# Second output projection of the last tokens by seven block products, with the weight sums made beside it

## The chip, the cores and the metric

The kernel runs on one core of one Trainium2 chip. The metric is the device time of one execution in microseconds (us), the median of three timed runs. TensorE is PE in the rows below (PEld its weight loads), VectorE is DVE, ScalarE is ACT, GpSimd is POOL; SP issues the DMAs.

## The reference, cut to what matters

```python
attn_out = _attn_ref(q, k, v)                     # window attention, 4 x 8 x 576 x 64
x = attn_out.transpose(0, 2, 1, 3).reshape(2304, 512)
h = 1.0 / (1.0 + np.exp(-(x @ moe_w_gate))) * (x @ moe_w_val)   # 2304 x 1536
x = h @ moe_w_out                                               # 2304 x 512
h = (x @ moe2_w_a) * (x @ moe2_w_b)                             # 2304 x 1536
out = h @ moe2_w_out                                            # 2304 x 512
```

Every matrix is multiplied as three products of a high and a low part (high by high, high by low, low by high), so that one 128-deep step of a product is three matmuls.

## The kernel before, in words

The 1536 hidden units are 12 blocks of 128 (`NF`). The 2304 tokens are nine blocks of 256. Five of them (`FRONT`) go through both MLPs in the first two thirds of the program, while the attention is computed and the weights are decoded from float64 words into high and low parts, which are saved to HBM (`kept`). The gate and value weights are also kept there in full precision (`kept[F, "f"]`), the output weights only as a pair (`kept[F, "o"]`).

The last four blocks, 1024 tokens, follow in a second part: first MLP (phase 0), some leftover work of token block 0, second MLP (phase 1). For each hidden block a *quad* (function `quad`) makes gate and value of the 1024 tokens by seven products of half-size blocks, each of six matmuls with 512 columns: products 1, 5, 6, 2, 7, 4, 3 in this order, into PSUM tiles `qa`, `qb`, `qc`. Between them `fill` takes jobs from the list `rest`: the output projection of the pair of hidden blocks before (`PAIR` is 2, so there are six pairs per MLP). `SLOTS` says how many jobs stand at which of the seven places. The combined weights of a quad (`wq`, made from `s`) are computed in `fetch` by POOL and ACT, some quads ahead.

In **phase 0** the projection of the first five pairs (`SEVEN`) is done by seven products as well (function `seven`): token halves x hidden blocks x halves of the output columns. It takes seven jobs for each of two row chunks, in two PSUM banks called `accx` and `accy`; a job is three matmuls of 512 columns and one or two additions of the bank to a result tile `res`, on DVE. Its operands are four sums of weights, summed earlier in `weight_sums` from high plus low and read back from HBM (`ks`), and four differences of hidden tiles (function `difference`): one DVE subtraction each, then a split into high and low by ACT and DVE (`t<-g,t`).

In **phase 1** the projection is the plain one (function `bank_sum`): for each of eight chunks of 128 tokens six matmuls with 512 columns, two hidden blocks of three, and one addition. The order of instructions on each engine is set by a scheduler from a simulated timeline; `in_order` ties PE to the order of the code, in phase 0 from its start to the sixth pair.

Of the kernel before, what the change touches and what calls it, by code (L numbers as in the profile page):

```python
# [21 lines left out]
def tile_window_attention_gated_mlps(ctx, tc, q, k, v, w1g, w1v, w1o, w2a, w2b, w2o, out):  # L22
    nc = tc.nc
    B, H, S, D = q.shape
    NT, DM = out.shape
    DFF = w1g.shape[1]
    P = 128
    NP = H // 2
    NF = DFF // P
    G = 3  # L30
    N = 256
# [3 lines left out]
    W = 2 * N  # L35
    CH = 2 * P
# [11 lines left out]
    dram = keep("dram", 1, space=bass.MemoryType.DRAM)  # L48
# [29 lines left out]
    for e in range(2):  # L78
        rows = slice(e * WIN, (e + 1) * WIN)
# [234 lines left out]
    SEVEN = NF // 2 - 1  # L314
    kept_sums = [dram.tile([P, 4, 2, CH], F32, tag=f"ks{p}", name=f"ks{p}") for p in range(SEVEN)]

    def weight_sums(p):

        fs = []
        for i in range(2):  # L320
            f = work.tile([P, DM], F32, tag="kq", bufs=3, name="oh")
            low = vs.tile([P, DM], F32, tag="v", bufs=3, name="ol")
            for j, t in enumerate((f, low)):
                nc.sync.dma_start(out=t, in_=kept[2 * p + i, "o"][:, j])
            fs.append((f, low))
# [65 lines left out]
    def decode_pair(F, i, nm):  # L391
        wf, wi = wordy.pop((F, nm))
        nc.vector.scalar_tensor_tensor(  # L393
            out=wf, in0=wf, scalar=SMALLEST, in1=wi.bitcast(F32), op0=ALU.is_ge, op1=ALU.mult
        )
        yield
        pair = wts.tile([P, 2, DM], F32R, tag=f"w{nm}", name=f"w{nm}")
        wh, wl = pair[:, 0, :], pair[:, 1, :]
        nc.scalar.activation(out=wh, in_=wf, func=AF.Copy)
        yield  # L400
        nc.vector.tensor_tensor(out=wl, in0=wf, in1=wh.bitcast(F32), op=ALU.subtract)
        parts.setdefault(F, {})[nm] = (wh, wl)
        pairs[F, nm] = pair
        yield
        if nm != "o":
            nc.sync.dma_start(out=kept[F, "f"][:, i], in_=wf)
            yield

    pairs = {}
# [244 lines left out]
    def in_order(since=0, engines=None):  # L654
        newest = {}
        for i in nc.cur_bb.bb.instructions[since:]:
# [6 lines left out]
                )  # L663
            newest[i.engine] = i.name

    def projection(ph, blk, work, begin, end):
        acc = [ps_acc.tile([P, 2, N], F32, tag="acc", name=f"acc{j}") for j in range(2)]
        for i, (w, h) in enumerate(work):
            project(ph, acc, w, h, i == 0, i == len(work) - 1)
        evacuate(ph, blk, acc, begin, end)  # L670
# [157 lines left out]

    def seven(res, begin, o, sums, b):


        half = lambda w, i: tuple(p[:, i * CH:(i + 1) * CH] for p in w)
        at = lambda i: tuple(sums[i // 2][:, i % 2, p] for p in range(2))
        a = {1: half(o[0], 0), 2: half(o[1], 0), 3: at(3), 4: half(o[1], 1), 5: at(0), 6: at(1), 7: at(2)}
        jobs = []
        for c in range(2):
            sl, bank, written = slice(c * P, (c + 1) * P), {}, set()

            def job(n, k, start, dsts, bank=bank, sl=sl, c=c, written=written):
                if k not in bank:  # L840
                    bank[k] = ps_acc.tile([P, W], F32, tag="acc", name=f"acc{k}")
                for m, (i, j) in enumerate(((0, 0), (0, 1), (1, 0))):
                    nc.tensor.matmul(  # L843
                        bank[k], lhsT=a[n][i][:, sl], rhs=b[n][j], start=start and m == 0, stop=m == 2,
                        skip_group_check=True,
                    )
                for d in dsts:
                    dst = res[d][:, c]
                    if begin and d not in written:
                        nc.scalar.activation(out=dst, in_=bank[k], func=AF.Copy)  # L850
                    else:
                        nc.vector.tensor_tensor(out=dst, in0=bank[k], in1=dst, op=ALU.add)
                    written.add(d)

            for args in (
                (1, "x", True, (0,)), (2, "y", True, (0,)), (6, "x", False, (1,)), (5, "y", True, (3,)),
                (7, "x", False, (2, 3)), (3, "y", False, (1,)), (4, "y", True, (2,)),
            ):
                jobs.append(lambda args=args, job=job: job(*args))
        return jobs  # L860

    def bank_sum(dst, pairs, begin):

# [125 lines left out]
    def fill(n=1):  # L989
        for _ in range(min(n, len(rest))):  # L990
            rest.pop(0)()
# [10 lines left out]
    PAIR = 2  # L1002
    SLOTS = {4: (1, 0, 1, 0, 1, 1, 0), 7: (0, 1, 1, 1, 2, 1, 1)}

    def slots(number):
        counts = SLOTS.get(number, (0, 0, 0, 0, number, 0, 0))
        return lambda i: fill(counts[i])

    y, hs, gs, pairs_done = {}, [], [], 0
    for n, (ph, fc) in enumerate(steps):  # L1010
        ahead(n + 1)
        w = fetched[n]
        if ph is None:
            hs.append((w, hidden(1, w, x[1, (0,)])))
            if fc == NF - 1:
                projection(1, 0, hs, False, True)
                hs = []
            continue
        if fc == 0:
            res = [accp.tile([P, 2, W], F32, tag="xacc", name=f"res{ph}{i}") for i in range(4)]  # L1020
        p = fc // PAIR
        by_seven = ph == 0 and p < SEVEN
        if by_seven and fc % PAIR == 0:
            g = quarter(0, 1, "g").bitcast(F32)
            g = [g[:, i] for i in range(2)]
            second = None
        else:
            g = [tmp.tile([P, W], F32, tag="hr", name=f"g{i}") for i in range(2)]
            second = None if by_seven else ((pairs_done - SEVEN) % 2, (fc + 1) % 2)
# [4 lines left out]
        hs.append((w["o"], quad(ph, w, x_ops, slots(number), g, second, between)))  # L1034
        if by_seven and len(hs) == 1:
            difference(ph, g[0], g[1], g[0], None)
            t1_of = lambda f=g[0]: t1.append(difference(0, f, None, None, wts.tile([P, 2, DM], F32R, tag="wa", name="t1")))
        if len(hs) < PAIR:
            continue
        if ph == 0 and p == SEVEN:  # L1040
            in_order(tied, (mybir.EngineType.PE,))
        fill(len(rest))
        pairs_done += 1
        begin, end = fc == PAIR - 1, fc == NF - 1
        if by_seven:
            sums = []
            for i in range(2):
# [9 lines left out]
            jobs = seven(res, begin, (o0, o1), sums, b)  # L1057

            def t4(before=jobs[1], b=b, args=(ph, g10, g10, g00)):
                before()  # L1060
# [60 lines left out]
```

## Time and profile before

| | us |
|---|---|
| median of three runs | 955.45 |
| lowest, highest | 952.73, 955.82 |
| the profiled execution | 954.69 |
| its span in the trace | 952.6 |
| PE busy | 936.5 |
| DVE busy | 664.8 |
| ACT busy | 469.4 |
| POOL busy | 301.9 |

The rows of the trace count from the start of the span; 2.1 us of the profiled execution lie around it. Phase 0 of the last tokens stands at about 600 to 755 us, phase 1 at about 757 to 953 us. Matmuls overlap: a row's own duration (390 ns for 512 columns) is longer than the distance from one start to the next, so the cost of a matmul is read from starts.

### The profile page before, as it was taken

How to read it: one execution, taken by the hardware profiler on the slowest of the kernel's cores; microseconds unless marked ns; L12 is line 12 of the kernel's file. 1: busy time of each engine (PE TensorE's matmuls, PEld its weight loads, DVE VectorE, ACT ScalarE, POOL GpSimd, SP SyncE). 2: the span in 40 equal slices, each digit the busy share in tenths (PEclk: the TensorE clock that was granted, in tenths of full speed). 3: DMA queues.
4: the chain of work that ended last, by engine and by line, in shares of the span. 5: the costliest groups of instructions: out<-in, count | busy, mean ns of one | idle time of the engine just before them, and what ended most of it. 6: DMA issues, size and time to landing. Idle time of an engine off the chain costs nothing.

```text
span 952.6 us, 15566 instructions
## 1 busy us (share of the span) xinstructions
PE 936.5 (98%) x5564; PEld 784.8 (82%) x5564; DVE 664.8 (70%) x1328; ACT 469.4 (49%) x1050; POOL 301.9 (32%) x318
## 2 busy tenths in 40 slices
PE   7899999999999999999999999999999999999998
PEld 6798888888888888888888888778888878888886
DVE  6997787875776874475788455788886774464655
ACT  7897555565545665544454333554433444432321
POOL 4543222332221222122013324444431435434400
PEclk9999999999999999999999999999999999999999
DMA  8987599975475754475695445555555664442212
GB/s 207 250 239 218 201 324 320 281 243 176 156 231 169 247 189 149 132 250 172 214 354 192 147 157 172 181 198 198 177 166 176 233 221 133 155 146 95 91 45 89
DMA packets 130045, 183.20 MB, mean 192 GB/s; under 512 B 62641, under 2 KB 87217, under 8 KB 129969
## 3 DMA queue, kind: packets, MB, share of 16 engines
q1 hardware_dynamic: 129968, 182.22, 59.1%
q8 instruction: 44, 0.72, 0.3%
q14 instruction: 33, 0.26, 0.1%
HBM read 117.44 MB, written 60.29 MB: 187 GB/s over the span
## 4 chain that ended last, share of the span: by engine, by line
PE 89%; DVE 5%; DMA 2%; issue 1%; POOL 1%; ACT 0%; SPq 0%; POOLq 0%; DVEq 0%; ACTq 0%
PE gps L428 15%; PE vps L428 15%; PE qa L753 13%; PE accm L528 9%; PE accq L866 8%; PE acc L481 7%; PE qb L753 7%; PE qc L753 3%; PE accy L843 3%; PE accx L843 2%; PE xps L228 2%; DMA oh<-ko 2%; PE sps L170 2%; PE tps L218 1%; POOL wi L387 1%
## 5 line engine op out<-in xcount | busy, mean ns | idle before, releaser
L387 POOL TENSOR_TENSOR wi<-wi,low 128x512 int32<-128x512 int32 x72 | 104.8, 1456 | 309.4 <-DVE wi L383 262.7
L428 PE MATMUL gps<-xh,wa 128*128 128x512 f32 (+1 forms) x584 | 169.3, 357 | 0.0
L428 PE MATMUL vps<-xh,wb 128*128 128x512 f32 (+1 forms) x584 | 167.4, 354 | 0.0
L738 POOL TENSOR_TENSOR wq<-s,wq 128x256 fp32r<-128x256 f32 x96 | 78.3, 821 | 138.3 <-ACT wq L737 138.0
L428 PEld LDWEIGHTS vps<-xh,wb 128*128 128x128 f32 x584 | 105.1, 189 | 16.1 <-ACT hr L448 0.4
L428 PEld LDWEIGHTS gps<-xh,wa 128*128 128x128 f32 x584 | 104.9, 189 | 16.0 <-issue 0.5
L428 PE MATMUL gps<-xl,wa 128*128 128x512 f32 (+1 forms) x292 | 103.0, 353 | 0.6 <-DVE xl L237 0.6
L428 PE MATMUL vps<-xl,wb 128*128 128x512 f32 (+1 forms) x292 | 102.7, 352 | 0.0
L528 PE MATMUL accm<-hh,wo 128*128 128x512 f32 (+1 forms) x296 | 83.5, 353 | 0.0
L771 ACT ACTIVATE r<-qa 128x512 f32<-128x512 f32 x72 | 42.7, 594 | 69.0 <-PE qa L753 65.7
L753 PE MATMUL qa<-op,wq 128*128 128x512 f32 x288 | 74.7, 390 | 0.7 <-ACT r L771 0.7
L481 PE MATMUL acc<-wo,hh 128*128 128x512 f32 x240 | 73.7, 392 | 0.2 <-DVE xacc L552 0.2
L753 PE MATMUL qb<-op,wq 128*128 128x512 f32 x288 | 73.6, 389 | 0.0
L393 DVE SCALAR_TENSOR_TENSOR ex<-ex,wi 128x512 f32<-128x512 f32 x72 | 49.8, 691 | 29.3 <-ACT ex L377 13.9
L735 POOL TENSOR_TENSOR s<-wf 128x256 f32<-128x256 f32 x48 | 37.5, 782 | 91.1 <-DMA wf<-kf 83.8
L753 PEld LDWEIGHTS qa<-op,wq 128*128 128x128 f32 x288 | 53.9, 188 | 12.3 <-ACT r L771 1.1
L753 PEld LDWEIGHTS qb<-op,wq 128*128 128x128 f32 x288 | 54.1, 188 | 11.2
L439 DVE SCALAR_TENSOR_TENSOR hl<-hr,hh 128x512 fp32r<-128x512 f32 (+1 forms) x73 | 48.1, 658 | 21.1 <-ACT hh L437 20.7
L437 ACT ACTIVATE hh<-hr 128x512 fp32r<-128x512 f32 (+1 forms) x73 | 40.2, 550 | 44.8 <-DVE hr L454 28.4
L428 PEld LDWEIGHTS gps<-xl,wa 128*128 128x128 f32 x292 | 55.2, 189 | 7.7 <-DVE xl L237 0.8
L428 PEld LDWEIGHTS vps<-xl,wb 128*128 128x128 f32 x292 | 55.2, 189 | 7.5
L528 PEld LDWEIGHTS accm<-hh,wo 128*128 128x128 f32 x296 | 52.7, 189 | 7.8 <-issue 0.2
(159 smaller groups left out, 1994.9 us busy)
## 6 DMA issues: line engine op xcount, KB each, us to landing
wa<-ka SPq DMA_DIRECT2D x27, 512.0 KB, 4.2
wb<-kb SPq DMA_DIRECT2D x27, 512.0 KB, 3.4
wo<-ko SPq DMA_DIRECT2D x27, 512.0 KB, 3.6
st_o<-in_moe_w_out_dram SPq DMA_DIRECT2D x24, 512.0 KB, 5.0
kf<-ex SPq DMA_DIRECT2D x48, 256.0 KB, 4.3
ka<-wa SPq DMA_DIRECT2D x24, 512.0 KB, 3.5
kb<-wb SPq DMA_DIRECT2D x24, 512.0 KB, 4.6
ko<-wo SPq DMA_DIRECT2D x24, 512.0 KB, 3.3
```

Source lines behind the costliest of these rows:

```text
L387: nc.gpsimd.tensor_tensor(out=wi, in0=wi, in1=low, op=ALU.add)
L393: nc.vector.scalar_tensor_tensor(out=wf, in0=wf, scalar=SMALLEST, in1=wi.bitcast(F32), op0=ALU.is_ge, op1=ALU.mult)
L428: nc.tensor.matmul(ps, lhsT=a[:, c * P:(c + 1) * P], rhs=b[:, c, :], start=(n == 0), stop=(n == 3 * NP - 1))
L437: nc.scalar.activation(out=hh, in_=hr, func=AF.Copy, scale=factor)
L439: nc.vector.scalar_tensor_tensor(out=hl, in0=hr, scalar=factor, in1=hh.bitcast(F32), op0=ALU.mult, op1=ALU.subtract)
L481: nc.tensor.matmul(ps, lhsT=a[:, m * P:(m + 1) * P], rhs=b, start=begin and n == 0 and (phase == 1 or m % 2 == 0), stop=end and n == 2 and ...
L528: nc.tensor.matmul(ps[:, m], lhsT=a[:, sl], rhs=b, start=k == 0, stop=k == total - 1)
L738: nc.gpsimd.tensor_tensor(out=t[:, 1], in0=s, in1=t[:, 0].bitcast(F32), op=ALU.subtract)
L753: nc.tensor.matmul(ps, lhsT=a[:, c * P:(c + 1) * P], rhs=b[:, c, :], start=first and n == 0, stop=n == 5, skip_group_check=True,)
L771: nc.scalar.activation(out=r, in_=ps, func=AF.Copy)
L843: nc.tensor.matmul(bank[k], lhsT=a[n][i][:, sl], rhs=b[n][j], start=start and m == 0, stop=m == 2, skip_group_check=True,)
L866: nc.tensor.matmul(ps, lhsT=a, rhs=b, start=n == 0, stop=n == len(pairs) - 1)
```

## The change

For the first five of the six pairs of phase 1 the projection becomes `seven` too. The tokens are the rows of the result there, so a hidden tile is the stationary operand and a block of weights, 256 columns wide, the moving one: a job is six matmuls of 256 columns, three for each of two token chunks. The sixth pair stays as it was. The differences of hidden tiles are made as in phase 0. The four sums of weights of a pair are made while its second quad runs (`sums_of`): two DMAs bring the full-precision output weights, which the decoding now writes to HBM for ten of the hidden blocks (`kept_out`), DVE makes four sums of 128x256, ACT and POOL split them. The function `behind` puts these instructions behind what stands before them in the code on their engine. PE is tied to the code's order in phase 1 also, from its second quad to its sixth pair.

```diff
+    kept_out = {F: dram.tile([P, DM], F32, tag=f"kf{F}", name=f"kf{F}") for F in range(NF, NF + 2 * SEVEN)}
...
         if nm != "o":
             nc.sync.dma_start(out=kept[F, "f"][:, i], in_=wf)
+            yield
+        elif F in kept_out:
+            nc.sync.dma_start(out=kept_out[F], in_=wf)
             yield
...
+    def behind(steps):
+        made = nc.cur_bb.bb.instructions
+        since, last = len(made), {}
+        if next(steps, steps) is steps:
+            return
+        for i in made[:since]:
+            last[i.engine] = i.name
+        for i in made[since:]:
+            if i.engine in last and i.engine != mybir.EngineType.SP:
+                tc.add_manual_dep(
...
-    def seven(res, begin, o, sums, b):
+    def seven(ph, res, begin, o, sums, b):
...
+                for r in range(2 if ph else 0):
+                    rows = slice((2 * c + r) * P, (2 * c + r + 1) * P)
+                    for m, (i, j) in enumerate(((0, 0), (0, 1), (1, 0))):
+                        nc.tensor.matmul(
+                            bank[k][:, r], lhsT=b[n][j][:, rows], rhs=a[n][i],
+                            start=start and m == 0 and r == 0, stop=m == 2, skip_group_check=True,
+                        )
                 for d in dsts:
-                    dst = res[d][:, c]
+                    i, j = divmod(d, 2)
+                    dst = res[2 * j + c][:, :, i * CH:(i + 1) * CH] if ph else res[d][:, c]
...
+    def sums_of(F):
+        p = (F - NF) // 2
+        if not spare:
+            spare.append(accp.tile([P, 2, W], F32, tag="xacc", name="osum"))
+        f = spare[0]
+        for i in range(2):
+            nc.sync.dma_start(out=f[:, i], in_=kept_out[F + i])
...
+        def steps():
+            yield
+            for n, (s, x, y, op) in enumerate((
+                (a22, a21, a22, ALU.add), (a21, a11, a21, ALU.subtract), (a11, a22, a11, ALU.subtract),
+                (a12, a12, a11, ALU.subtract),
+            )):
+                nc.vector.tensor_tensor(out=s, in0=x, in1=y, op=op)
+                if n % 2:
+                    yield
+            for n, s in enumerate((a22, a11, a21, a12)):
+                t = sums[n // 2][:, n % 2]
+                nc.scalar.activation(out=t[:, 0], in_=s, func=AF.Copy)
+                nc.gpsimd.tensor_tensor(out=t[:, 1], in0=s, in1=t[:, 0].bitcast(F32), op=ALU.subtract)
+                yield
...
+        def at(i):
+            fill(counts[i])
+            behind(also)
...
+        if fc == (1 if ph else 0):
+            tied = len(nc.cur_bb.bb.instructions)
...
-        by_seven = ph == 0 and p < SEVEN
+        by_seven = p < SEVEN
...
+        if by_seven and ph and len(hs) == 1:
+            sums, also = sums_of(NF + 2 * p)
...
-        if ph == 0 and p == SEVEN:
+        if p == SEVEN:
             in_order(tied, (mybir.EngineType.PE,))
```

Three places show what the change moves. The first is PE where phase 1 begins, in the first two quads, which have no jobs between their products. In the program before, `wq_8479` to `wq_8484` belong to the first quad, `wq_8559` to `wq_8569` to the second, `wq_8651` and `wq_8656` to the third:

```order
L753 MATMUL qa<-op_8370,wq_8479 128x512 x6
L753 MATMUL qa<-op_8375,wb 128x512 x6
L753 MATMUL qb<-op_8378,wq_8484 128x512 x6
L753 MATMUL qa<-op_8365,wq_8559 128x512 x6
L753 MATMUL qb<-op_8360,wq_8651 128x512 x6
L866 MATMUL accq<-wo,hh 128x512 x4
L753 MATMUL qc<-op_8355,wa 128x512 x6
L866 MATMUL accq<-wo,hl 128x512 x2
L753 MATMUL qa<-op_8370,wq_8564 128x512 x6
L753 MATMUL qa<-op_8352,wa 128x512 x6
L753 MATMUL qa<-op_8375,wb 128x512 x6
L753 MATMUL qb<-op_8378,wq_8569 128x512 x6
```

The same place of PE now, with `wq_8494` to `wq_8504` of the first quad and `wq_8579` to `wq_8589` of the second:

```order
L774 MATMUL qa<-op_8385,wq_8494 128x512 x6
L774 MATMUL qa<-op_8390,wq_8499 128x512 x6
L774 MATMUL qa<-op_8395,wb 128x512 x6
L774 MATMUL qa<-op_8385,wq_8579 128x512 x6
L774 MATMUL qc<-op_8375,wa 128x512 x6
L774 MATMUL qb<-op_8398,wq_8504 128x512 x6
L774 MATMUL qa<-op_8390,wq_8584 128x512 x6
L774 MATMUL qa<-op_8395,wb 128x512 x6
L774 MATMUL qb<-op_8398,wq_8589 128x512 x6
L774 MATMUL qa<-op_8372,wa 128x512 x6
```

Products of the third quad no longer stand among those of the second, whose products 7 and 4 (`wq_8584`, `wb`), both into the tile `qa`, now follow each other directly.

The second place is PE in one quad of the running phase, from its product 5 on. Before:

```order
L753 MATMUL qb<-op_8360,wq_8869 128x512 x6
L753 MATMUL qc<-op_8355,wa 128x512 x6
L753 MATMUL qa<-op_8352,wa 128x512 x4
L866 MATMUL accq<-wo,h_8638 128x512 x2
L753 MATMUL qa<-op_8370,wq_8754 128x512 x6
L866 MATMUL accq<-wo,h_8638 128x512
L866 MATMUL accq<-wo,h_8731 128x512 x3
L866 MATMUL accq<-wo,h_8638 128x512 x3
L866 MATMUL accq<-wo,h_8731 128x512 x3
L753 MATMUL qa<-op_8352,wa 128x512 x2
L753 MATMUL qa<-op_8375,wb 128x512 x6
L753 MATMUL qb<-op_8378,wq_8759 128x512 x6
```

PE in the same quad now:

```order
L774 MATMUL qb<-op_8380,wq_9107 128x512 x6
L874 MATMUL accx<-wo,hh 128x256
L874 MATMUL accx<-wo,hl 128x256
L874 MATMUL accx<-wo,hh 128x256 x2
L874 MATMUL accx<-wo,hl 128x256
L874 MATMUL accx<-wo,hh 128x256
L774 MATMUL qa<-op_8385,wq_9112 128x512 x6
L874 MATMUL accy<-wo,hh 128x256
L874 MATMUL accy<-wo,hl 128x256
L874 MATMUL accy<-wo,hh 128x256 x2
L874 MATMUL accy<-wo,hl 128x256
L874 MATMUL accy<-wo,hh 128x256
```

Groups of six 256-column matmuls stand between the products, seven groups in a quad, where groups of 512-column matmuls stood.

The third place is the end of a pair's second quad, on DVE and POOL. DVE before, from the multiplication by `qa` on:

```order
L781 TENSOR_TENSOR g_9262<-qa,g_9262 128x512
L811 TENSOR_TENSOR g_9263<-qb,r_9295 128x512
L439 SCALAR_TENSOR_TENSOR hl<-g_9262,hh 128x512
L781 TENSOR_TENSOR g_9263<-r_9318,g_9263 128x512
L801 TENSOR_TENSOR g_9387<-qc,r_9398 128x512
L870 TENSOR_TENSOR res_8574<-accq,res_8574 128x512
L439 SCALAR_TENSOR_TENSOR h_9356<-g_9263,h_9356 128x512
L870 TENSOR_TENSOR res_8574<-accq,res_8574 128x512
```

DVE now, from the same operation on:

```order
L802 TENSOR_TENSOR g_9271<-qa,g_9271 128x512
L884 TENSOR_TENSOR res_8595<-accy,res_8595 128x2x256
L444 SCALAR_TENSOR_TENSOR hl<-g_9271,hh 128x512
L832 TENSOR_TENSOR g_9272<-qb,r_9310 128x512
L884 TENSOR_TENSOR res_8593<-accy,res_8593 128x2x256
L802 TENSOR_TENSOR g_9272<-r_9344,g_9272 128x512
L840 TENSOR_TENSOR g_9125<-g_9272,g_9125 128x512 x2
L444 SCALAR_TENSOR_TENSOR h_9412<-g_9272,h_9412 128x512
L840 TENSOR_TENSOR g_9271<-g_9271,g_9125 128x512
L444 SCALAR_TENSOR_TENSOR t_9404<-g_9125,t_9404 128x512
L884 TENSOR_TENSOR res_8592<-accx,res_8592 128x2x256
L444 SCALAR_TENSOR_TENSOR t_9408<-g_9125,t_9408 128x512
```

Three subtractions (L840) and the splits of `h` and `t` now stand between the products of a pair and the first addition of the next (`res<-accx`). POOL before, making the weights of coming quads:

```order
L738 TENSOR_TENSOR wq_9369<-s_9367,wq_9369 128x256
L735 TENSOR_TENSOR s_9382<-wf,s_9372 128x256
L738 TENSOR_TENSOR wq_9374<-s_9372,wq_9374 128x256
L738 TENSOR_TENSOR wq_9379<-s_9377,wq_9379 128x256
L735 TENSOR_TENSOR s_9492<-wf 128x256
L735 TENSOR_TENSOR s_9497<-s_9492,wf 128x256
L738 TENSOR_TENSOR wq_9384<-s_9382,wq_9384 128x256
L735 TENSOR_TENSOR s_9502<-wf 128x256
L738 TENSOR_TENSOR wq_9494<-s_9492,wq_9494 128x256
```

POOL now, with the four low parts of the sums of weights (`<-osum`) among them:

```order
L756 TENSOR_TENSOR s_9438<-wf,s_9428 128x256
L923 TENSOR_TENSOR s_9275<-osum,s_9275 128x256
L759 TENSOR_TENSOR wq_9430<-s_9428,wq_9430 128x256
L756 TENSOR_TENSOR s_9569<-wf 128x256
L923 TENSOR_TENSOR s_9275<-osum,s_9275 128x256
L759 TENSOR_TENSOR wq_9435<-s_9433,wq_9435 128x256
L756 TENSOR_TENSOR s_9574<-s_9569,wf 128x256
L923 TENSOR_TENSOR s_9276<-osum,s_9276 128x256 x2
L759 TENSOR_TENSOR wq_9440<-s_9438,wq_9440 128x256
L756 TENSOR_TENSOR s_9579<-wf 128x256
```

Each pair has four such instructions more on POOL, between the weights of its coming quads.

## Rows read from the trace of the kernel before

**Rows 1.** The page: busy time of each engine over the span.
```profile
PE 936.5 (98%) x5564; PEld 784.8 (82%) x5564; DVE 664.8 (70%) x1328; ACT 469.4 (49%) x1050; POOL 301.9 (32%) x318
```

**Rows 2.** Chain that ended last, second MLP: start us, us, what.
```profile
832.27 2.72 PE accq L866 x12
...
862.19 2.72 PE accq L866 x12
```

**Rows 3.** Stretches: us; PE, PEld, DVE, ACT, POOL busy us (instructions); PEclk, DMA, GB/s.
```profile
661.65:690.35 28.70, 28.70 (x127) 23.54 (x126) 24.38 (x38) 12.97 (x26) 12.94 (x17) 1.00 0.54 183
...
832.19:862.11 29.92, 29.92 (x134) 24.77 (x133) 16.48 (x23) 8.68 (x19) 12.70 (x17) 1.00 0.41 141
```

**Rows 4.** Timeline of PE: start us, us, line, operation, shapes, count.
```profile
732.23 1.52 PE L753 MATMUL qb<-op,wq 128*128 128x512 f32 x6
733.59 0.39 PE L843 MATMUL accx<-hh,wo 128*128 128x512 f32 x1
...
734.27 0.28 PE L428 MATMUL gps<-xh,wa 128*128 128x256 f32 x1
...
735.71 1.55 PE L753 MATMUL qa<-op,wq 128*128 128x512 f32 x6
737.09 0.39 PE L843 MATMUL accy<-hh,wo 128*128 128x512 f32 x1
```

**Rows 5.** Timeline of PE where the second MLP begins; in brackets idle and releaser.
```profile
777.95 1.65 PE L753 MATMUL qa<-op,wq 128*128 128x512 f32 x6 [0.69 <-ACT r L771]
780.29 1.65 PE L753 MATMUL qa<-op,wb 128*128 128x512 f32 x6 [0.69 <-ACT r L771]
```

**Rows 6.** Timeline of PE, first MLP: `accx<-t,s` of pairs 1, 2 and 4.
```profile
604.84 0.73 PE L843 MATMUL accx<-t,s 128*128 128x512 f32 x2 [0.82 <-DVE t L439]
...
634.07 0.94 PE L843 MATMUL accx<-t,s 128*128 128x512 f32 x3
...
691.71 0.84 PE L843 MATMUL accx<-t,s 128*128 128x512 f32 x3
```

**Rows 7.** Timeline of DVE before the last of those rows.
```profile
688.92 1.23 DVE L819 TENSOR_TENSOR g<-g,g 128x512 f32<-128x512 f32 x1
690.08 0.68 DVE L852 TENSOR_TENSOR res<-accx,res 128x512 f32<-128x512 f32 x1
690.68 1.28 DVE L439 SCALAR_TENSOR_TENSOR t<-g,t 128x512 fp32r<-128x512 f32 x2
```

**Rows 8.** Timeline of DVE early in the second block of a pair, first MLP.
```profile
674.21 0.69 DVE L852 TENSOR_TENSOR res<-accx,res 128x512 f32<-128x512 f32 x1 [0.68 <-PE accx L843]
676.25 0.69 DVE L852 TENSOR_TENSOR res<-accy,res 128x512 f32<-128x512 f32 x1 [1.35 <-PE accy L843]
677.68 0.69 DVE L801 TENSOR_TENSOR g<-qc,r 128x512 f32<-128x512 f32 x1 [0.74 <-PE qc L753]
```

**Rows 9.** Timeline of DVE in the second MLP.
```profile
838.35 1.23 DVE L439 SCALAR_TENSOR_TENSOR hl<-g,hh 128x512 fp32r<-128x512 f32 x1
839.51 1.22 DVE L781 TENSOR_TENSOR g<-r,g 128x512 f32<-128x512 f32 x1
840.65 0.68 DVE L801 TENSOR_TENSOR g<-qc,r 128x512 f32<-128x512 f32 x1
```

**Rows 10.** Timeline of POOL over the same stretch.
```profile
838.30 0.74 POOL L738 TENSOR_TENSOR wq<-s,wq 128x256 fp32r<-128x256 f32 x1 [4.59 <-ACT wq L737]
839.12 1.06 POOL L735 TENSOR_TENSOR s<-wf,s 128x256 f32<-128x256 f32 x1
```

**Rows 11.** DVE groups, 440 to 560 us: count, busy us, mean ns, idle before.
```profile
L336 DVE TENSOR_TENSOR osum<-oh 128x256 f32<-128x256 f32 x10 | 5.0, 528 | 4.6 <-PE xps L228 4.6
...
L336 DVE TENSOR_TENSOR osum<-oh,osum 128x256 f32<-128x256 f32 x5 | 2.1, 415 | 0.0
```

**Rows 12.** The page: DMA issues, KB each, median us to landing.
```profile
kf<-ex SPq DMA_DIRECT2D x48, 256.0 KB, 4.3
```

**Rows 13.** Waits of ACT, 440 to 600 us: us in total, times, longest.
```profile
ACT ex L377 <- DMA kf<-ex: 9.4, 4, 3.7
```

More of the change, by code (lines that the diff above doesn't have):

```diff
@@ L664, in in_order @@
             newest[i.engine] = i.name
+    def behind(steps):
[8 more added lines that the diff above has]
+                tc.add_manual_dep(
+                    i, last[i.engine],
+                    mybir.DependencyInfo(mybir.DependencyClass.NoSync, mybir.DependencyReason.DATA), reason="behind",
+                )
     def projection(ph, blk, work, begin, end):
@@ L841, in job @@
                     bank[k] = ps_acc.tile([P, W], F32, tag="acc", name=f"acc{k}")
+                    if ph:
+                        bank[k] = bank[k].rearrange("p (r n) -> p r n", r=2)
                 for m, (i, j) in enumerate(((0, 0), (0, 1), (1, 0))):
[L843 to L846, printed above, removed]
+                    if ph == 0:
+                        nc.tensor.matmul(
+                            bank[k], lhsT=a[n][i][:, sl], rhs=b[n][j], start=start and m == 0, stop=m == 2,
+                            skip_group_check=True,
+                        )
+                for r in range(2 if ph else 0):
+                    rows = slice((2 * c + r) * P, (2 * c + r + 1) * P)
+                    for m, (i, j) in enumerate(((0, 0), (0, 1), (1, 0))):
+                        nc.tensor.matmul(
+                            bank[k][:, r], lhsT=b[n][j][:, rows], rhs=a[n][i],
+                            start=start and m == 0 and r == 0, stop=m == 2, skip_group_check=True,
+                        )
                 for d in dsts:
-                    dst = res[d][:, c]
+                    i, j = divmod(d, 2)
+                    dst = res[2 * j + c][:, :, i * CH:(i + 1) * CH] if ph else res[d][:, c]
                     if begin and d not in written:
@@ L860, in seven @@
         return jobs
+    spare = []
+    def sums_of(F):
[5 more added lines that the diff above has]
+            nc.sync.dma_start(out=f[:, i], in_=kept_out[F + i])
+        if p % 2:
+            sums = [xs.tile([P, NP, N], F32R, tag=f"x{h}0", name=f"s{h}").rearrange("p (n h) c -> p n h c", n=2) for h in "hl"]
+        else:
+            sums = [late["sums"].tile([P, 2, 2, CH], F32R, tag="t", name=f"s{i}") for i in range(2)]
+        (a11, a21), (a12, a22) = ((f[:, i, 0:CH], f[:, i, CH:]) for i in range(2))
+        def steps():
[12 more added lines that the diff above has]
+                yield
+        return sums, steps()
     def bank_sum(dst, pairs, begin):
@@ L1003, in tile_window_attention_gated_mlps, with slots @@
     SLOTS = {4: (1, 0, 1, 0, 1, 1, 0), 7: (0, 1, 1, 1, 2, 1, 1)}
-    def slots(number):
+    def slots(number, also=iter(())):
         counts = SLOTS.get(number, (0, 0, 0, 0, number, 0, 0))
-        return lambda i: fill(counts[i])
+        def at(i):
+            fill(counts[i])
+            behind(also)
+        return at
     y, hs, gs, pairs_done = {}, [], [], 0
@@ L1021, in tile_window_attention_gated_mlps @@
         p = fc // PAIR
-        by_seven = ph == 0 and p < SEVEN
+        by_seven = p < SEVEN
+        also = iter(())
         if by_seven and fc % PAIR == 0:
@@ L1028, in tile_window_attention_gated_mlps @@
             g = [tmp.tile([P, W], F32, tag="hr", name=f"g{i}") for i in range(2)]
-            second = None if by_seven else ((pairs_done - SEVEN) % 2, (fc + 1) % 2)
+            second = None if by_seven else (0, (fc + 1) % 2)
         gs.append(g)
@@ L1033, in tile_window_attention_gated_mlps @@
         number = -(-len(rest) // (PAIR - len(hs)))
-        hs.append((w["o"], quad(ph, w, x_ops, slots(number), g, second, between)))
+        if by_seven and ph and len(hs) == 1:
+            sums, also = sums_of(NF + 2 * p)
+        hs.append((w["o"], quad(ph, w, x_ops, slots(number, also), g, second, between)))
         if by_seven and len(hs) == 1:
             difference(ph, g[0], g[1], g[0], None)
-            t1_of = lambda f=g[0]: t1.append(difference(0, f, None, None, wts.tile([P, 2, DM], F32R, tag="wa", name="t1")))
+            t1_of = lambda f=g[0], ph=ph: t1.append(difference(ph, f, None, None, wts.tile([P, 2, DM], F32R, tag="wa", name="t1")))
         if len(hs) < PAIR:
             continue
-        if ph == 0 and p == SEVEN:
+        if p == SEVEN:
             in_order(tied, (mybir.EngineType.PE,))
@@ L1045, in tile_window_attention_gated_mlps @@
         if by_seven:
-            sums = []
-            for i in range(2):
+            whole(also)
+            if ph == 0:
+                sums = []
+            for i in range(0 if ph else 2):
                 t = late["sums"].tile([P, 2, 2, CH], F32R, tag="t", name=f"s{i}")
@@ L1056, in tile_window_attention_gated_mlps @@
             b = {1: b11, 2: b21, 3: b22, 5: t1[0], 6: t2, 7: t3}
-            jobs = seven(res, begin, (o0, o1), sums, b)
+            jobs = seven(ph, res, begin, (o0, o1), sums, b)
             def t4(before=jobs[1], b=b, args=(ph, g10, g10, g00)):
```

## The prediction, made before the changed kernel ran

> **What bounds the kernel now.** I read the engine shares first: PE is busy in 936.5 of 952.6 us, DVE in 664.8 [rows 1]. Then the chain of waits: in the second MLP of the last tokens it runs through PE alone, and repeats every 29.92 us, from 832.27 to 862.19 [rows 2]. A pair of hidden blocks is 84 matmuls in its two quads and 48 in its projection, 132 of 512 columns; 29.92 / 132 = 0.2267 us, which is also the distance of starts in a timeline: six from 732.23 to 733.59 [rows 4]. So PE streams there without a hole, and what the change does to PE's own work is worth its full price. Third, the stretches: in one such pair DVE is busy 16.48 of 29.92 us, ACT 8.68, POOL 12.70; in a pair of phase 0, which projects by seven products already, DVE is busy 24.38 of 28.70 us and ACT 12.97 [rows 3]. The question is therefore whether DVE can carry that load in phase 1 also, with the sums of weights on top.
>
> **PE's own work.** Removed are 5 pairs x 48 matmuls of 512 columns, 48 x 0.2267 = 10.88 us a pair. Added are 5 x 84 of 256 columns (seven products, two row chunks each, two token chunks in each, three matmuls). Twelve such matmuls start between 734.27 and 735.71, 0.120 us each [rows 4]; 84 x 0.120 = 10.08 us. That is 0.80 us a pair, **4.0 us** in all: an eighth of the columns is saved, but 256 columns cost more than half of 512. By the Trainium skill (TensorE: Matmul & The Clock Gate, Back-to-back issue gap) a matmul takes N / 2.4 + 2.5 ns, 215.8 and 109.2 ns here; the sum by that would be 240 x 0.2158 - 420 x 0.1092 = 5.9 us. The rows are 11 ns above it at both widths, which costs the narrow kind twice as much per column, so the rows decide.
>
> A change of width costs a little: after the narrow matmuls six wide ones take from 735.71 to 737.09, 1.38 us instead of 1.36 [rows 4]. A quad has six places where a narrow group is followed by a wide product (`accy` and `accx` of jobs 5 and 7 stand together), ten quads 60: 60 x 0.02 = **1.2 us** given back. Its bounds are 0 and, at 0.03, 1.8.
>
> **The start of phase 1.** In a quad without jobs, product 4 follows product 7 in the same PSUM tile and waits for ACT to copy it: 777.95 to 780.29 is 2.34 us for six matmuls worth 1.36 [rows 5], 0.98 lost. Before, the scheduler put products of the third quad into that gap of the second quad; PE is now tied to the code from the second quad on, and the order of PE shows product 4 directly behind product 7 there. I add one such wait, **1.0 us**; 0 if ACT were earlier, which nothing suggests.
>
> The first pair also has to make its differences while DVE is still behind. In phase 0 the same job (6, `accx<-t,s`) of the first pair waited 0.82 us for the split `t`; in the second pair the row has no idle before it and is 0.10 longer than the one at 691.71 [rows 6]. For phase 1 I take **0.4 us** between 0 and 1.0: there is no tanh on ACT in its way, but POOL is busier.
>
> **The running pairs.** This is the term that decides. DVE gets what phase 0 has (eight more additions a pair, four subtractions, three splits) and four sums of 128x256, 0.415 to 0.528 us each [rows 11], 1.7 to 2.1 us. From phase 0's 24.38 us that is 26 to 26.5 us in a pair that would last 84 x 0.2267 + 84 x 0.12 = 29.12 us. The sums themselves stand where DVE has air: early in the second quad of a phase-0 pair it idles 0.68, 1.35 and 0.74 us before three operations [rows 8]. I cost them at nothing there; without that air they would be 2 us a pair on DVE.
>
> The tight place is the next quad's start. In phase 0 job 6 starts on PE at 691.71 [rows 6]; it needs the split `t` that DVE begins at 690.68 and ends some 0.65 later, and the addition of job 1 that begins at 690.08 and ends at 690.76, since both use one bank [rows 7]. Margins: about 0.4 and 0.95 us. In phase 0 a pair loses 28.70 - 126 x 0.2267 = 0.14 us [rows 3]. In phase 1 the order of DVE puts that addition behind the split. The split gains 0.6 us of margin, the addition loses as much: about 0.4 us is left for it, and 0.1 more because two narrow jobs before it are longer by 0.04 each.
>
> Against this stand four more instructions on POOL a pair, and they meet DVE. At 838.35 and 839.51 DVE operations that read two SBUF tiles took 1.23 and 1.22 us while POOL ran from 838.30 to 840.18 [rows 9, 10]; the next one, reading PSUM, took 0.68 [rows 9]. So one meeting costs DVE 0.54 us. The low parts of the sums are ready for POOL toward the end of the second quad, just before the weights of the coming quad, and DVE's row of three subtractions and splits stands there: all of it SBUF to SBUF. Four meetings are 2.2 us, none is 0. With 0.5 us of margin a pair loses between 0.14 and 1.8 us. I take 0.6, since of POOL's four operations the first two probably meet DVE at operations on PSUM (L832 and the addition after it, which stand first in the order). Four pairs: **2.4 us**, bounds 0.6 and 7.2.
>
> The Trainium skill (SBUF — State Buffer, SBUF: two separate sides) says that DVE operations with two SBUF inputs and POOL share a port pair as an exclusive lock, and that the loser waits out the whole instruction. By that rule an uncovered meeting would cost up to POOL's 0.74 us; the rows show 0.54. With 0.74, four meetings would be 3.0 us and the loss 2.5 a pair. The rival of that name below is the same mechanism at the rows' price.
>
> **What I cost at nothing.** ACT gets 3 splits and 4 copies a pair; at phase 0's 12.97 us [rows 3] plus the copies it stays far below the pair's 29 us. The two loads of 256 KB a pair stand in SP's order among the weights of coming quads, where phase 0 has its two loads of sums; a transfer of this size lands 4.3 us after its issue [rows 12], and a quad is 14.6 us. If a load came late, DVE would wait with its additions queued behind, and PE behind those. Ten more writes of 256 KB leave in the first half. There ACT has waited 4 times, 9.4 us together, until such a write released a decoding tile [rows 13]. Ten more would be up to 23 us on ACT, which is busy half the time [rows 1]; PE follows only where its jobs run out. I take 0. Their other end is the rival on decoding below.
>
> **The sum**, against the profiled execution of 954.69 us: -4.0 + 1.2 + 1.0 + 0.4 + 2.4 = +1.0, 955.7 us. The median of the runs shown, 955.45, lies 0.8 above that execution, so I put the forecast at 956.4: no difference that can be told, for 0.3 per cent, 2.9 us, is about what a measurement of this kernel can tell from no change.
>
> **Rivals.**
> *The gain survives.* DVE keeps up as in phase 0 and the changes of width vanish in PE's queue. Then -4.0 + 0 + 0.4 + 0 + 0.6 = -3.0, about 952.4, at the edge of faster; 951.5 with nothing given back. For it: phase 0 loses 0.14 a pair at 85 per cent of DVE. Against: the start's wait, which the order shows, has to go too.
> *DVE and POOL meet every time* (slower). The price is 1.8 us a pair in place of 0.6: -4.0 + 1.2 + 1.0 + 1.0 + 7.2 = +6.4, about 961.9. It decides from a loss of 1.1 us a pair, which is three meetings of four. For it: both meetings in [rows 9] happened. Against: POOL's low parts wait for ACT copies, which may spread them.
> *Decoding is held up* (slower). If the ten writes hold ACT as the four of [rows 13] did, 2.35 us each, and PE loses a fifth of it, 4.7 us are added: 961. Against: PE is busy 98 per cent now with 48 such writes made [rows 1, 12].
> That the change doesn't do what it says I exclude: the order shows the narrow jobs in place.
>
> **How the numbers follow.** Forecast 0.55, gain survives 0.15, meetings 0.22, decoding 0.08. So faster by over 0.3 per cent 0.15, within it 0.55, slower 0.30. The range from 951.8 to 961.5 leaves out a part of the first rival and the worst of the second and third.
>
> **What would show it.** Starts of the narrow matmuls 0.12 us apart; a first pair with three waits of `qa` for ACT instead of two; a pair's period between 29.2 and 31 us, with PE's idle before `accx<-s,t` put down to DVE; DVE busy about 26 to 28 us of it, its subtractions 1.2 us where POOL runs. The prediction is wrong if PE is held at other places: by a load of `osum`, or before 600 us.

## The result, and the profile of the changed kernel

| | before | after |
|---|---|---|
| median of six runs, us | 954.43 | 959.03 |
| lowest, highest | 952.31, 955.82 | 957.35, 961.29 |
| the profiled execution, its span | 954.69, 952.6 | 960.97, 959.2 |
| DVE busy | 664.8 | 726.1 |
| POOL busy | 301.9 | 320.4 |

The ratio is 1.0054 [1.0042, 1.0066]: the change makes the kernel slower by 0.5 per cent, some 5 us. That lies in the range that was forecast, but not in its likeliest case. The page of the changed kernel, busy time of each engine, answers to [rows 1]:

```profile
PE 937.2 (98%) x5744; PEld 790.4 (82%) x5744; DVE 726.1 (76%) x1423; ACT 486.0 (51%) x1085; POOL 320.4 (33%) x338
```

Half a per cent is lost in a PE that is as busy as before, so the place has to be looked up. Waits of PE in the whole span (us in total, times, longest):

```profile
PE vps L433 <- ACT hr L453: 2.1, 1, 2.1
PE qa L774 <- ACT r L792: 2.1, 3, 0.7
...
PE accx L874 <- DVE t L444: 1.9, 1, 1.9
...
PE accx L874 <- DVE res L884: 1.5, 5, 0.4
```

Four rows; the first is a place in the first MLP of other tokens, and two of the three waits of `qa` were there before [rows 5]. The third row is job 6 of the first pair, the dearest place with what follows it. The timeline of PE there:

```profile
797.29 0.28 PE L874 MATMUL accx<-s,t 128*128 128x256 f32 x1
799.48 1.20 PE L874 MATMUL accx<-s,t 128*128 128x256 f32 x5 [1.91 <-DVE t L444]
800.48 2.76 PE L774 MATMUL qa<-op,wq 128*128 128x512 f32 x6
803.04 0.95 PE L874 MATMUL accy<-s,t 128*128 128x256 f32 x6
```

The first matmul of the job starts, the second waits for the low part of `t`: 797.41 to 799.48, 2.07 us of idle. Behind it six matmuls of 512 columns take 2.56 us from start to start instead of 1.39. The stretches (us; PE, PEld, DVE, ACT, POOL busy; PEclk, DMA, GB/s) show the granted clock there:

```profile
793.00:797.30 4.30, 4.30 (x27) 3.75 (x25) 4.27 (x5) 3.42 (x8) 4.30 (x5) 1.00 0.15 36
797.30:799.48 2.18, 0.27 (x2) 0.00 (x0) 2.18 (x3) 0.79 (x2) 2.18 (x3) 1.00 1.02 396
799.48:800.50 1.02, 1.02 (x6) 1.02 (x7) 1.02 (x2) 0.00 (x0) 0.94 (x2) 0.65 0.16 48
800.50:803.00 2.50, 2.50 (x7) 1.96 (x7) 1.87 (x4) 0.60 (x1) 1.86 (x2) 0.50 0.18 52
```

The granted clock fell to 0.50, its lower level of 1.2 GHz, just after the idle, and not in it. From 799.48 to 803.83 that costs 1.65 us on top: 0.40 in the job, 1.17 in the product, 0.08 in the next job. The same rows show DVE and POOL busy all the time up to there. Their timelines, DVE first:

```profile
793.74 2.27 DVE L840 TENSOR_TENSOR g<-g,g 128x512 f32<-128x512 f32 x2
795.93 1.22 DVE L444 SCALAR_TENSOR_TENSOR h<-g,h 128x512 fp32r<-128x512 f32 x1
797.07 1.22 DVE L840 TENSOR_TENSOR g<-g,g 128x512 f32<-128x512 f32 x1
798.22 2.35 DVE L444 SCALAR_TENSOR_TENSOR t<-g,t 128x512 fp32r<-128x512 f32 x2
```

```profile
795.41 1.19 POOL L759 TENSOR_TENSOR wq<-s,wq 128x256 fp32r<-128x256 f32 x1
796.57 1.18 POOL L923 TENSOR_TENSOR s<-osum,s 128x256 fp32r<-128x256 f32 x1
797.71 1.17 POOL L756 TENSOR_TENSOR s<-wf 128x256 f32<-128x256 f32 x1
798.84 1.18 POOL L759 TENSOR_TENSOR wq<-s,wq 128x256 fp32r<-128x256 f32 x1
```

Six DVE operations in a row start 1.14 us apart, where one alone takes 0.60; POOL's start as far apart. In the prediction's words every one of them is a meeting at 0.54.

The running pairs are read best from the start of the last job (`accy<-wo,t`) in one pair's first quad to the same job in the next pair's: such a stretch holds a pair's second quad and the next pair's first, where the jobs of the new differences begin. A quad without any wait is 14.68 us. The stretches of the third, fourth and fifth pair, in the columns of [rows 3]:

```profile
838.05:868.69 30.64, 30.04 (x170) 25.69 (x168) 28.82 (x42) 11.72 (x25) 16.90 (x20) 1.00 0.49 154
868.69:899.34 30.65, 30.05 (x170) 25.70 (x169) 28.82 (x42) 11.71 (x25) 17.30 (x20) 1.00 0.47 157
899.34:928.70 29.36, 29.36 (x170) 25.81 (x169) 26.30 (x42) 10.86 (x22) 9.51 (x11) 1.00 0.20 65
```

This is the clearest view of the case. DVE carries the same 42 instructions in all three. In the last of them POOL has no weights left to make, 11 instructions instead of 20, and DVE needs 2.52 us less for the same work, 4.7 meetings of 0.54; PE then has no wait at all, 29.36 = 2 x 14.68. The same subtraction in the one and the other (DVE):

```profile
858.36 1.23 DVE L840 TENSOR_TENSOR g<-g,g 128x512 f32<-128x512 f32 x1
```

```profile
918.52 0.68 DVE L840 TENSOR_TENSOR g<-g,g 128x512 f32<-128x512 f32 x1
```

The first place in the list of waits lies at 279 us. ACT, PE and the issues on SP there:

```profile
273.30 0.64 ACT L442 ACTIVATE hh<-hr 128x512 fp32r<-128x512 f32 x1 [1.83 <-DVE hr L455]
278.07 0.66 ACT L376 ACTIVATE low<-st_o 128x512 int32<-128x512 uint32 x1 [4.13 <-DMA st_o<-in_moe_w_out_dram]
278.63 0.59 ACT L453 ACTIVATE hr<-gps 128x512 f32<-128x512 f32 x1
```

```profile
279.27 0.50 PE L433 MATMUL vps<-xh,wb 128*128 128x512 f32 x1 [2.10 <-ACT hr L453]
```

```profile
268.17 1.39 SPq L411 DMA_DIRECT2D kf<-ex  x1
...
270.20 0.54 SPq L354 DMA_DIRECT2D st_o<-in_moe_w_out_dram  x1
```

One of the ten new writes (L411) leaves two microseconds ahead of a load of raw weights. That load lands at 277.98, 7.8 us after its issue. ACT stands in its queue at the decoding step that reads it, with the copy that PE waits for behind. In the kernel before, the load took 5.9 us, and ACT did the same step 1.6 us earlier though the load was issued 0.3 us later:

```profile
270.47 0.54 SPq L352 DMA_DIRECT2D st_o<-in_moe_w_out_dram  x1
```

```profile
276.45 0.67 ACT L374 ACTIVATE low<-st_o 128x512 int32<-128x512 uint32 x1 [1.76 <-DMA st_o<-in_moe_w_out_dram]
277.02 0.58 ACT L448 ACTIVATE hr<-gps 128x512 f32<-128x512 f32 x1
```

### The profile page after: what moved, and what is told of

Read it like the earlier page. It is cut to its first block, busy times and chain, and to the rows that moved or that the text cites. A ratio compares the mean times of both kernels' runs of the same rounds, so it can differ in the third digit from the quotient of the medians.

```text
span 959.2 us, 16156 instructions
## 1 busy us (share of the span) xinstructions
PE 937.2 (98%) x5744; PEld 790.4 (82%) x5744; DVE 726.1 (76%) x1423; ACT 486.0 (51%) x1085; POOL 320.4 (33%) x338
## 4 chain that ended last, share of the span: by engine, by line
PE 76%; DVE 13%; DMA 4%; ACT 3%; issue 2%; POOL 1%; SPq 0%; DVEq 0%; ACTq 0%; POOLq 0%
PE gps L433 14%; PE vps L433 14%; PE qa L774 11%; PE acc L486 8%; PE accm L533 6%; PE qb L774 5%; PE accy L867 3%; PE qc L774 3%; PE accq L932 2%; DMA kf<-ex 2%; PE accy L874 2%; PE accx L867 2%; PE accx L874 2%; PE xps L228 2%; DVE g L840 1%
## 5 line engine op out<-in xcount | busy, mean ns | idle before, releaser
L389 POOL TENSOR_TENSOR wi<-wi,low 128x512 int32<-128x512 int32 x72 | 101.9, 1415 | 310.9 <-DVE wi L385 254.2
L756 POOL TENSOR_TENSOR s<-wf 128x256 f32<-128x256 f32 x48 | 42.6, 888 | 106.8 <-DMA wf<-kf 91.9
L884 DVE TENSOR_TENSOR res<-accy,res 128x512 f32<-128x512 f32 x76 | 52.1, 686 | 20.2 <-PE accy L867 12.0
```

Of the source, the lines that this page charges most:

```text
L389: nc.gpsimd.tensor_tensor(out=wi, in0=wi, in1=low, op=ALU.add)
L756: nc.gpsimd.tensor_tensor(out=s, in0=x, in1=y, op=op)
```

## The experiments

All are compared with the kernel before, measured beside them (median 953.9 to 954.1 in the three sets).

**The writes alone.**

```diff
+    kept_out = {F: dram.tile([P, DM], F32, ...) for F in range(NF, NF + 2 * SEVEN)}
+        elif F in kept_out:
+            nc.sync.dma_start(out=kept_out[F], in_=wf)
+            yield
```

> The kernel before, with the ten writes of decoded out-matrices (kf, 256 KB each) added and nothing else changed. Theory: the writes cost one wait of PE in the first half, as the wait of vps on ACT's hr at 279.27 in the changed kernel's trace (gap 2.26 us): 1.5 to 2.5 us slower than the kernel before, and the trace shows that wait between 250 and 300 us. Rival A, the writes are free and the wait came from elsewhere: within 0.7 us. Rival B, the prediction's decoding held up at 2.35 us a write: about 4.7 us slower.

Median 956.53, ratio 1.0024 [1.0008, 1.0039]: about 2.3 us. The wait is there, at the same place, ACT and PE:

```profile
278.12 0.66 ACT L376 ACTIVATE low<-st_o 128x512 int32<-128x512 uint32 x1 [4.30 <-DMA st_o<-in_moe_w_out_dram]
```

```profile
279.32 0.50 PE L433 MATMUL vps<-xh,wb 128*128 128x512 f32 x1 [2.01 <-ACT hr L453]
```

So the writes carry a price of their own, and it is one wait rather than ten. It doesn't come every time: of the six variants of the changed kernel below that keep the writes, the profiles show gaps of 1.02, 0.40 and 0.37 us there (2.26 in the changed kernel), and three none.

**Ready sums, no writes.** The two loads of `osum` and the making of sums are replaced by two loads of `kept_sums[p]`, and `kept_out` is empty.

> The changed kernel without the making of sums and without the ten writes: each pair of phase 1 loads two ready tiles of sums (those of phase 0's weights, so the second MLP's values are others) in place of the two osum loads, four additions or subtractions on DVE, four copies on ACT and four low parts on POOL. Theory (POOL's four operations and DVE's sums are what holds the pairs): PE idle before the first pair's job 6 falls from 2.07 to below 1 us, the granted clock stays at 1.00, a running pair lasts 29.4 to 29.7 us instead of 30.6, and the time is 953.5 to 955. Rival (the eight additions, the differences and splits alone fill DVE, the sums are bystanders): first pair and periods stay as they are, and only the writes' 2 us are gone: 957.

Median 955.37, ratio 1.0007 [0.9996, 1.0017]. PE at the first pair's job 6, and the third to fifth running pair:

```profile
794.84 0.28 PE L874 MATMUL accx<-s,t 128*128 128x256 f32 x1
795.80 0.85 PE L874 MATMUL accx<-s,t 128*128 128x256 f32 x5 [0.69 <-DVE t L444]
```

```profile
832.30:862.26 29.96, 29.74 (x169) 25.75 (x168) 25.76 (x38) 10.36 (x21) 13.11 (x16) 1.00 0.53 176
862.26:892.22 29.96, 29.73 (x169) 25.74 (x168) 25.74 (x38) 10.36 (x21) 13.14 (x16) 1.00 0.53 175
892.22:921.58 29.36, 29.36 (x169) 25.83 (x168) 23.73 (x38) 9.54 (x18) 5.67 (x7) 1.00 0.19 65
```

The theory holds for the first pair, 0.84 us of idle instead of 2.07 and no fall of the clock, and in part for the running pairs: they are 0.68 us shorter, but 29.96 us is over the 29.4 to 29.7 that it gave. Even with sums for nothing the structure only breaks even: a pair is still 29.96 long where plain products take 29.92 [rows 2].

**POOL's part twice.** `for _ in range(2):` before the low part on POOL.

> The changed kernel with each of POOL's four low parts of sums a pair made twice (the same operation again, same result); DVE, ACT, PE and the DMAs have the work they had. Theory (DVE is late because POOL runs beside its row of SBUF operations at a pair's end): the idle before job 6 grows, by 0.5 to 1 us in the first pair and 0.3 to 1 us in the running pairs, but not in the last pair by seven, where POOL has nothing more to do: 961 to 964. Rival (DVE's own amount of work sets the pace, POOL is a bystander): 958.5 to 959.7, as the changed kernel.

Median 963.14, ratio 1.0100 [1.0084, 1.0116]. The same three pairs:

```profile
838.65:869.80 31.15, 30.04 (x169) 25.70 (x168) 29.31 (x42) 11.72 (x25) 21.52 (x24) 1.00 0.48 151
869.80:900.95 31.15, 30.04 (x169) 25.71 (x168) 29.31 (x42) 11.72 (x25) 21.32 (x24) 1.00 0.47 156
900.95:930.47 29.52, 29.52 (x169) 25.80 (x168) 27.83 (x42) 10.80 (x22) 13.02 (x16) 1.00 0.20 63
```

DVE's 42 instructions take 0.49 us longer though DVE got nothing more to do, and the pair lasts 0.50 longer; the pair where POOL runs out of work early loses 0.16. The DMA share is that of the changed kernel (0.48 and 0.20), so the added time is not that of the transfers, which also thin out in the last of the three. The theory missed the first pair, whose idle did not grow (2.04 us), and the second, which lasts 1.4 us longer, not 0.3 to 1. POOL is no bystander.

**DVE's sums twice.** `for d in (sums[n // 2][:, n % 2, 0], s):` before the addition on DVE.

> The changed kernel with each of DVE's four additions for the sums of a pair made twice (first into a part of the tile that ACT overwrites): 1.7 us a pair more on DVE, nothing else. Theory (the sums stand where DVE has air, early in a pair's second quad, as the prediction costed them): running pairs as they are, within 0.3 us each, and the first pair up to 1.7 us later, since its four extra additions fall into the row at its end: 959.5 to 961.5. Rival (DVE has no air anywhere): 1.7 us in each of four or five pairs, 965 to 968.

Median 968.34, ratio 1.0152 [1.0139, 1.0165]: my theory fell here. The rival's price of 1.7 us came out in the third and fourth pair (1.6 and 1.7 longer); the fifth is 1.0 longer and the second not at all, and the time lies just above the rival's range. The third pair, and PE in the middle of its second quad:

```profile
840.60:872.80 32.20, 30.72 (x169) 25.61 (x168) 30.82 (x46) 11.73 (x25) 17.66 (x20) 1.00 0.46 148
```

```profile
853.82 0.39 PE L874 MATMUL accy<-sl,h 128*128 128x256 f32 x1 [0.33 <-DVE res L884]
```

The pair is 1.6 us longer, nearly what DVE got more, and PE now also waits in the second quad, where the first four sums had cost nothing (14.68 us in every one). DVE's timeline of that quad in the changed kernel has one idle of 0.20 us behind the first sums, and here none: the air of [rows 8] was nearly used up before. The first pair's job 6 waited 3.55 us.

**Low parts on DVE.** `nc.vector` for `nc.gpsimd` in the same line.

> The changed kernel with the four low parts of a pair's sums made by DVE instead of POOL: DVE gets 4 x 0.42 = 1.7 us a pair more, and POOL's four operations a pair are gone. Theory (meetings with POOL are the price, 0.54 us each): first pair's idle gets shorter by up to 1 us and the running pairs stay or gain 0.5 us: 955 to 959. Rival (DVE's amount of work is the price, whoever meets it): up to 1.7 us a pair more, 962 to 967.

Median 962.65, ratio 1.0088 [1.0068, 1.0108]: the rival. Four meetings at 0.54 are not worth 1.7 us of DVE's time.

**A later split.** In phase 1 the split of `g11` for job 3 is tied behind the split for job 6 and the addition of job 1.

```diff
-            b22 = difference(ph, g11, None, None, quarter(0, 0, "h"))
...
             def t4(...):
                 before()
+                b[3] = difference(ph, f, None, None, quarter(0, 0, "h"))   # DVE's part behind t2's split and job 1's addition
```

> The changed kernel with one change of DVE's order in phase 1: the split of the difference that job 3 reads (h) stands behind the split that job 6 reads (t) and behind the addition of job 1, instead of ahead of both. Theory (it is the order in DVE's row at a pair's end, not the amount of its work, that makes job 6 late): the 0.5 us of idle before job 6 of each running pair go, the first pair's 2.07 us fall to 0.9 or less and the clock stays at 1.00: 3 to 5 us faster than the changed kernel, 954 to 956. Rival (DVE has no air, so that the next job in the row is late instead): the idle moves to jobs 7 and 3, no more than 1 us gained, 958 to 959.

Median 960.26, ratio 1.0076 [1.0054, 1.0097], not distinguishable from the changed kernel: the rival. In the first pair job 6 hardly waits any more, the next one does (PE):

```profile
800.37 0.97 PE L874 MATMUL accy<-s,t 128*128 128x256 f32 x6 [1.78 <-DVE res L884]
```

Of the running pairs the third is 0.58 us shorter than in the changed kernel and the fourth 0.08. The third:

```profile
835.39:865.45 30.06, 29.84 (x170) 25.80 (x168) 28.23 (x42) 11.81 (x25) 17.75 (x20) 1.00 0.49 156
```

The time shows no gain from it. The profiled execution is the fastest of six, 957.65, and the others have a lower mean clock (last section), which the two theories had not reckoned with.

**No tie of PE in phase 1.** `if ph == 0 and p == SEVEN:` before `in_order`.

> The changed kernel with PE tied to the order of the code in phase 0 only, so that products of the next quad may fill the waits at the start of phase 1 again. Theory: one wait of qa for ACT (0.98 us) goes, and where the scheduler also puts other products before the first pair's job 6, part of its 2.07 us idle: 1 to 3 us faster than the changed kernel, 956 to 958. Rival: without the tie the running pairs' jobs slide together and wait for one another: slower than the changed kernel, 960 to 964.

Median 969.01, ratio 1.0153 [1.0133, 1.0173]. The tie, which I had charged with a microsecond, saves ten. In the order of PE that the scheduler makes, products of later quads move ahead, jobs fall behind, and PE waits for DVE at one job after another (waits of PE); even the wait that I meant to remove stays (`qa` for ACT, four times):

```profile
PE accy L874 <- DVE res L884: 4.0, 6, 1.3
PE qa L774 <- ACT r L792: 2.4, 4, 0.7
```

**First pair plain.** `by_seven = p < SEVEN if ph == 0 else 0 < p < SEVEN`, PE tied from `fc == 3`.

> The changed kernel with the first pair of phase 1 projected by plain products again and the other four by seven; PE is tied from the fourth quad on. Theory (the first pair pays because its differences fall on DVE and POOL where both still make the operands and weights of the start): the 2.07 us of idle before its job 6, the stretch at the low clock behind it (1.2 us) and one wait of qa for ACT (1.0 us) go, 0.45 us of PE's saving goes with them: 3.5 to 4 us faster than the changed kernel, about 955. Rival (whichever pair is first by seven pays): the second pair then shows the 2 us idle and the clock's fall: 957.5 to 959.

Median 955.67, ratio 1.0016 [1.0006, 1.0026]: 3.6 us better than the changed kernel, as the theory said. Its profile also lacks the wait at 279 us, though the writes are kept; how much of the 3.6 us that is, isn't shown. The pair that is first by seven now waits 0.89 us from start to start instead of 2.07, and the clock stays at 1.00 (PE):

```profile
824.67 0.95 PE L874 MATMUL accx<-sh,t 128*128 128x256 f32 x6 [0.70 <-DVE res L884]
```

**Sums made in the first half.** `weight_sums` runs over all ten pairs, two of its steps at a time; phase 1 loads `kept_sums[SEVEN + p]`; no `kf` writes of out-matrices.

> The changed kernel with the sums for phase 1 made in the first half, from the kept parts, as those of phase 0 are, and loaded ready; no kf writes of out-matrices, no osum. Theory (phase 1 is then what the run with ready sums was, and DVE has air in the first half for 5 x 4.4 us more): 955 to 956, no wait of vps for hr near 279 us. Rival (DVE has no air in the first half, where it is over 90 per cent busy between 480 and 520 us): PE waits there 3 to 6 us, 958 to 961.

Median 955.47, ratio 1.0014 [1.0004, 1.0023], as the theory said: no wait of `vps` shows near 279 us, and DVE had the air in the first half.

**All three, and the two without the late split.**

> The changes of the last three together: first pair plain, late split, sums made in the first half. Theory (each removes a loss of its own): 4 pairs x -0.45 us of PE's work, no idle at a pair's start, no extra wait at phase 1's start: 1 to 2 us faster than the kernel before, 952 to 953.5. Rival (the losses share a cause, so that two of the three give nothing on top): 954.5 to 956.

> First pair plain and sums made in the first half, without the late split of the run with all three. Theory (the late split only moves the wait to a later job of the same row, as its own run showed): the same as the run with all three within 0.5 us, 953 to 954.5. Rival (once POOL's part of the sums is gone, the order at a pair's end decides): 0.5 us a running pair slower, about 955.5.

With the late split 953.47, ratio 0.9999 [0.9990, 1.0008]; without it 954.30, ratio 1.0003 [0.9994, 1.0013]. Their running pairs, with it first:

```profile
833.61:863.12 29.51, 29.51 (x169) 25.86 (x168) 25.24 (x38) 10.37 (x21) 13.13 (x16) 1.00 0.53 178
```

```profile
831.51:861.47 29.96, 29.74 (x170) 25.73 (x168) 25.75 (x38) 10.38 (x21) 13.14 (x16) 1.00 0.53 175
```

Once DVE has air again (25 of 30 us), the order in its row does matter, as the second rival said: 0.45 us in each of two pairs, where the full row of the changed kernel gave 0.58 and 0.08. In the times this can't be told, for the two intervals overlap. The 1 to 2 us under the kernel before that the first theory gave did not come: the ratio is 0.9999. Neither version is faster than the kernel before. I found none that is.

## Why the prediction was right and where it was wrong

What the profiled executions add up to, by the prediction's own terms:

| term, us | predicted | in the trace |
|---|---|---|
| PE's own work with changes of width | -2.8 | -2.8 |
| third wait of `qa` at the start | +1.0 | +1.0 |
| first pair | +0.4 | +3.7 |
| four running pairs | +2.4 | +3.2 |
| decoding | 0 | +2.2 |
| sum | +1.0 | +7.3 |

The spans differ by 6.6 us and the executions by 6.3. The rest of the span is two short waits at the start of phase 1 (+0.7, below), a shorter wait at the tail (-0.5), and other places ahead of phase 1 (-0.9 in sum, 0.7 of it in the first 60 us). The profiled execution of the changed kernel was 1.9 us above its median, so not all of these terms are in the others. Its mean granted clock is 0.998. Four of the six executions have 0.999 or 1.000, and they are the four fastest (957.35 to 959.33): a stretch at the low clock as long as the profiled one is not in them. Without its 1.65 us the difference would be 4.6, which is that of the medians.

**PE's own work** was right in both parts: 29.36 us for a pair without waits against 29.92 [rows 2] is 0.56, times five 2.8. The forecast was 4.0 less 1.2 for the changes of width. PE's timeline shows both, 0.71 us for six narrow matmuls and 1.39 for six wide ones between them:

```profile
856.19 0.28 PE L874 MATMUL accx<-wo,hh 128*128 128x256 f32 x1
...
856.90 1.55 PE L774 MATMUL qa<-op,wq 128*128 128x512 f32 x6
858.29 0.28 PE L874 MATMUL accy<-wo,hh 128*128 128x256 f32 x1
```

**The start** was right in the wait that it named: three waits of `qa` for ACT, 0.98 to 0.99 us lost at the third. It had no term for two shorter ones: 0.45 us inside product 4 of the first quad, for an operand from DVE, and 0.28 ahead of product 7 of the second (PE):

```profile
779.52 1.45 PE L774 MATMUL qa<-op,wb 128*128 128x512 f32 x5 [0.18 <-DVE op L716]
```

Untied, PE waits there four times, so taking the tie away is no way around the term.

**The first pair** is the step that failed most. Its term of 0.4 and even its bound of 1.0 were taken from the first pair of phase 0, with "but POOL is busier" as a remark and no price on it. The price of a meeting stood further below, and the row to apply it to was in the order of DVE: six SBUF operations, from the last multiplication (L802) to the split `t`, before job 6 can go on. All of them met POOL, 6 x 0.54 = 3.2 us, of which 2.07 reached PE. What the forecast had no term for at all is the fall of the clock behind this idle, 1.65 us where it came.

**The running pairs** were 3.2 us instead of 2.4, between the forecast and the rival named after the meetings: 0.65, 1.28, 1.28 and 0. The mechanism was the one named, idle before `accx<-s,t` put down to DVE, subtractions at 1.23. The size was off because DVE's load was: 26.3 us of work is what the forecast had (26 to 26.5), but the 2.5 us of meetings belong into that sum, not only into the margin of one job. At 28.8 of 30.6 us DVE has next to no room: 0.49 us more through POOL made the pair 0.50 longer, and 2.00 us more through the doubled sums 1.56. The pair's period less DVE's busy time is 1.82, 1.84 and 1.4 us in the changed kernel and these two.

**The sums at nothing** held for the second quad (14.68 us in every pair), but only for the amount that was there.

**Decoding** was put at zero, and as a rival at 2.35 us a write on ACT. Place and cause were different: ACT waits for a load that lands late, not for a decoding tile, and once, not ten times. That a load might come later when 256 KB more leave just ahead of it was not weighed at all; "before 600 us" stood rightly among the signs of an error. That the delay of the load comes from sharing the DMA engines with the write is argued from the two issue times; only that the writes bring the wait is shown.

**The range** held in part by luck. Its upper end, 961.5, was drawn for running pairs that meet POOL every time and for decoding tiles that hold ACT. What took the time up to 959 was in good part the first pair, whose bound was 1.0, and the one late load, put at 0.

**The Trainium skill**, page SBUF — State Buffer, section SBUF: two separate sides, says of the port pair that DVE and POOL share that it is held for a whole instruction and the other blocks. The alternation above, one operation each in 1.14 us, agrees with that order. Its price does not follow from POOL's duration of 0.74: what POOL takes from DVE is 1.14 - 0.60 = 0.54, as [rows 9] had it.

## What to carry to other kernels

Where two engines delay each other as DVE and POOL do here, put the meetings into the load of the engine that is delayed, before asking whether a margin at one place covers it; a stretch in which the other engine is silent gives the price for nothing. A saving of an eighth in matmul columns is small change (0.56 of 29.92 us here) when narrower matmuls, additions and weight sums come with it. And price the first round of a pipeline from what runs beside it there, not from the first round of a similar loop.

## What the runs showed of the hardware

DVE operations with two SBUF inputs (0.60 us from start to start alone) and POOL's 128x256 operations alternate strictly when both have a row to do, with starts 1.14 us apart on each engine; PSUM-reading operations of DVE in between kept their 0.68.

The granted clock fell to 1.2 GHz after 2.07 us of idle in the changed kernel and stayed there until about 803 us. Waits of 0.98 us never did that, and neither did 1.97 us of idle in the profiled execution of the late-split run, whose stretch without a matmul (us, PE busy, PEclk, DMA, GB/s) reads:

```profile
799.00:800.00 1.00, 0.00 (x0) 1.00 0.94 291
```

So the length of one wait doesn't settle it. With the low parts on DVE the clock fell after two waits close together, 0.75 us ahead of a matmul at 796.37 and 1.36 ahead of the next at 798.12 (by the profile's count of idle, in which the two above are 1.91 and 1.78):

```profile
799.00:801.00 2.00, 2.00 (x6) 0.50 0.98 381
```

The other five executions of the late-split run have a mean granted clock of 0.996 to 0.998, against 1.000 in the profiled one, so it fell in them; where is not shown.
